# Cluster attention and token mixing: score operands kept in the rows where casts write them, and the two heads of a pair in the two halves of TensorE's rows

## The chip, the cores and the metric

The kernel runs on one core of one Trainium2 chip. The metric is the device time of one execution in microseconds; the number for the kernel before is the median of three runs. All arithmetic of the reference is done on the core; the host only transposes and reshapes inputs and output.

## The reference

```python
# q, k, v: (4, 8, 768, 64); centroids: (8, 16, 64); batch 4, 8 heads, 768 tokens
q_assign = np.argmax(np.einsum('bhsd,hcd->bhsc', q_n, c_n), axis=-1)
k_assign = np.argmax(np.einsum('bhsd,hcd->bhsc', k_n, c_n), axis=-1)
mask = q_assign[:, :, :, None] == k_assign[:, :, None, :]
scores = scale * np.matmul(q, k.transpose(0, 1, 3, 2))
scores = np.where(mask, scores, -1000000000.0)
scores = scores - np.max(scores, axis=-1, keepdims=True)
attn = np.exp(scores)
attn = attn / (np.sum(attn, axis=-1, keepdims=True) + 1e-09)
attn_out = np.matmul(attn, v)
...
# x: the eight heads side by side, (4, 768, 512)
theta = x @ w_theta
cos_t, sin_t = (np.cos(theta), np.sin(theta))
zr = x * cos_t
zi = x * sin_t
yr = np.einsum('ts,bsd->btd', w_tok_r, zr)
yi = np.einsum('ts,bsd->btd', w_tok_i, zi)
u = x + yr + yi
return u + np.maximum(u @ w_ch, 0.0)
```

Each query attends only to keys whose nearest centroid is its own. The inputs are float32, and w_theta and w_tok_i are scaled by about 5.5.

## The kernel before

**Stages.** Attention comes first, for 16 pairs of heads (two heads of one batch, 64 channels each, so a pair fills 128 rows). Then token mixing runs batch by batch: theta in six tiles of 128 tokens (`theta`, L602), the two mixing products (`mix`, L677), and the channel product with its relu (`channel`, L719). Values that need float32's precision are split into a high and a low float32r part (hi, lo) whose products are added in PSUM: hi·hi + hi·lo + lo·hi.

**One pair.** Its 768 x 768 scores are cut into twelve *units*: two halves a of 384 queries by six tiles i of 128 keys. A unit holds both heads j. `scores` (L356) makes for each head a 128 x 384 tile of scores with keys in rows, and ScalarE's exponential writes it to `at` (L367). GpSimd adds the `at` of three units into `acc` (L374). `weighted` (L405), three units later (`LAG`), multiplies by v into `av`, two units at a time. `sums` (L376) adds the columns of `acc` on TensorE into `sm`; `se` is the sum, VectorE inverts it (L394, 128 x 384), a DMA writes four rows of it to DRAM (`sd`, L397), two more read it back to all rows (`rb`, L400), and `normalise` (L419) multiplies and stores the pair to `xT_d`. These stages stand at the units `SUMS` and `NORM` of the next pair.

**Shift and mask in the product.** A one-hot of the 16 clusters, scaled by 2^60 on the side of the keys, is part of the product's rows: a pair of tokens of one cluster adds 0, any other a huge negative number. The row maximum that is subtracted comes from a cheaper product of hi parts with queries in rows (`row_max`, L325, tile `m`), which VectorE reduces (L341) into `nm`; `shift_row` (L345) transposes `nm` (tile `mt`), and a DMA puts it as one row into the score operands. `row_max` runs `LEAD` = 11 units ahead of `scores`, and shift rows are made four units ahead of their first use (five for the first pair).

**Operand tiles.** TensorE sums over up to 128 rows in one product. hi·hi (64 rows), parts of the other terms and the 16 one-hot rows are packed for each head into t1q/t1k (112 rows: 64 of hi·hi, 32 of hi·lo, 16 of one-hot) and t2q/t2k (97 rows: lo·hi, the rest of hi·lo, the shift row against a row of ones). So a score tile takes two products, and a maximum, which uses t1 alone, takes one for each half of the keys. Casts write hi and lo in rows (head, channel); `spread` (L307) moves them into place with 16 DMAs per pair on SyncE's queue, and four more (L272) move the one-hot rows.

**Assignment.** `assign` (L217) loads q and k of a pair, multiplies with the normalised centroids (`lg`, four column groups), transposes (`lt`, three transposes), takes the maximum on VectorE, breaks ties, writes the one-hot `oh`, transposes it in six steps into `ot`, and one ScalarE instruction of 64 x 768 writes it to `oht` (L265). Its stages stand at units `A_UNITS` of earlier pairs.

**Order.** The code writes instructions unit by unit, and `in_order` (L457) chains those of one engine in just that order. In the loop at L525 each unit issues score products and maxima of both heads in turn, then `weighted`, then whatever `todo` holds for the unit. In the units before the first score TensorE also gets two idle products a step (`WARM`).

**PSUM.** Of eight banks four are two double banks for `m`, one is `av`, and three (tag "bank") serve sc, lg, lt, ot, mt and sm in turn.

**Weights.** Float weights arrive as pairs of 32-bit words of float64, which VectorE and ScalarE turn into float32 (`to_f32`, L112), and `split_w` cuts into hi and lo. `early_weights` (L428) does eight chunks (w_theta, and two of six tiles each of w_r and w_i) beside attention, 18 units apart. `late` (L585) does the other w_r and w_i, and w_ch in eight chunks of 256 columns, while batch 0 mixes.

## Time and profile before

| what | value |
|---|---|
| median of 3 runs | 863.19 us (862.38 to 864.5) |
| the profiled execution | 865.01 us, of which 863.2 us are the span in the profile |
| mean granted TensorE clock | 0.976 |
| busy time by stage, 0 to 43 us (before the first score) | PE 24.59, VectorE 18.32 |
| 43 to 490 us (attention) | PE 429.74 of 447, VectorE 311.38, GpSimd 326.59, ScalarE 253.62 |
| 490 to 600 us | PE 94.86 of 110, VectorE 92.84 |
| HBM | read 45.15 MB, written 12.68 MB |

How to read it: the span runs from the first to the last instruction. PE is TensorE's products and PEld its loads of stationary operands, which overlap products. A busy PE need not be at its peak, because a product's end is modelled and includes the drain of the array; the distance between the starts of two products is what a step costs. An engine's mean share hides that the stages have different limits, so each stage is read by itself. "sc<-t1q,t1k" is a product that writes the tile sc from the operands t1q and t1k, and L365 is its line.

### The profile page before, as it was taken

What the parts mean: (1) busy time and instruction counts of PE and PEld (TensorE: products, weight loads), DVE (VectorE), ACT (ScalarE), POOL (GpSimd) and SP (SyncE); (2) the same over time, 40 slices, a digit from 0 to 9 for tenths busy, and PEclk for the clock granted to TensorE, in tenths of its full rate; (3) what the DMA queues carried; (4) which work ended last, traced back from release to release, by engine and by line L of the source; (5) the groups of instructions that cost most, each with busy time, mean ns of one, the idle gap of its engine ahead of it and who ended that gap; (6) DMA issues with size and microseconds to landing.
All of it is one profiled execution on the core that took longest, in us unless ns stands there. A gap on an engine that the chain in (4) does not pass through costs nothing.

```text
span 863.2 us, 12659 instructions
## 1 busy us (share of the span) xinstructions
PE 809.2 (94%) x4637; PEld 596.4 (69%) x4637; DVE 513.4 (59%) x665; ACT 398.9 (46%) x798; POOL 470.4 (54%) x303
## 2 busy tenths in 40 slices
PE   3799999999998989999999999868999999999998
PEld 1476565656565656565656678658888988899998
DVE  4476768786766687776654498994323442344222
ACT  3155565556554655565555655452333333333220
POOL 4157776977596668876867555546122512251231
PEclk9899999999998999999999999997999999999999
DMA  8856658675877496757631154321200120010001
GB/s 204 207 149 155 177 143 195 178 187 150 183 188 169 124 218 157 200 143 180 165 102 56 38 185 145 89 83 55 93 1 1 51 96 2 1 45 29 1 13 63
DMA packets 44942, 99.67 MB, mean 115 GB/s; under 512 B 8400, under 2 KB 19408, under 8 KB 44496
## 3 DMA queue, kind: packets, MB, share of 16 engines
q1 hardware_dynamic: 44288, 98.27, 42.8%
q8 instruction: 37, 0.61, 0.3%
q10 hardware_dynamic: 592, 0.59, 0.3%
q14 instruction: 25, 0.20, 0.1%
HBM read 45.15 MB, written 12.68 MB: 67 GB/s over the span
## 4 chain that ended last, share of the span: by engine, by line
PE 60%; DMA 13%; DVE 12%; issue 4%; ACT 4%; SPq 3%; POOL 2%; ACTq 0%; POOLq 0%; DVEq 0%
PE y L687 18%; PE sc L365 10%; PE av L411 9%; PE tp L620 6%; PE m L337 5%; PE cy L710 4%; DMA t2k<-rawk 3%; PE cp L710 3%; DMA t1k<-hik 2%; PE sm L384 2%; SPq L317 2%; DMA rawk<-in_kT_dram 2%; DVE wtmp L135 2%; POOL acc L374 2%; DMA rb<-sd 1%
## 5 line engine op out<-in xcount | busy, mean ns | idle before, releaser
L341 DVE TENSOR_REDUCE nm<-m 128x1 f32<-128x768 f32 x192 | 180.8, 950 | 134.8 <-PE m L337 131.8
L367 ACT ACTIVATE at<-sc 128x384 f32<-128x384 f32 x384 | 178.3, 491 | 129.7 <-PE sc L365 104.1
L374 POOL TENSOR_TENSOR acc<-at,at 128x768 f32<-128x768 f32 x64 | 120.0, 1875 | 101.5 <-ACT at L367 101.3
L365 PE MATMUL sc<-t1q,t1k 112*128 112x384 f32 x384 | 146.6, 382 | 8.5 <-ACT oht L265 4.4
L411 PE MATMUL av<-at,vt 128*64 128x384 f32 x768 | 147.5, 506 | 0.0
L337 PE MATMUL m<-t1k,t1q 112*128 112x384 f32 x384 | 139.2, 363 | 7.9 <-DVE nm L341 5.3
L365 PE MATMUL sc<-t2q,t2k 97*128 97x384 f32 x384 | 132.6, 345 | 2.5 <-DMA t2q<-mr 2.4
L374 POOL TENSOR_TENSOR acc<-acc,at 128x768 f32<-128x768 f32 x64 | 121.6, 1901 | 18.2 <-ACT at L367 15.5
L365 PEld LDWEIGHTS sc<-t1q,t1k 112*128 112x128 f32 x384 | 73.6, 192 | 69.4 <-issue 33.1
L641 POOL TENSOR_TENSOR zlc<-ab,zhc 128x512 fp32r<-128x512 f32 x24 | 32.1, 1336 | 162.1 <-ACT zhc L639 162.1
L411 PEld LDWEIGHTS av<-at,vt 128*64 128x64 f32 x768 | 47.2, 137 | 59.7 <-issue 59.5
L337 PEld LDWEIGHTS m<-t1k,t1q 112*128 112x128 f32 x384 | 77.3, 201 | 12.1 <-DVE nm L341 7.7
L365 PEld LDWEIGHTS sc<-t2q,t2k 97*128 97x128 f32 x384 | 73.6, 192 | 3.7 <-DMA vt<-in_v_dram 2.7
L624 DVE TENSOR_SCALAR kk<-tp 128x512 int32<-128x512 f32 x24 | 16.5, 686 | 93.8 <-PE tp L620 93.8
L701 POOL TENSOR_TENSOR ul<-xT,uh 128x384 fp32r<-128x384 f32 (+1 forms) x36 | 33.8, 963 | 34.4 <-ACT uh L700 34.2
L687 PE MATMUL y<-wi_hi,zls 128*128 128x512 f32 (+1 forms) x216 | 52.4, 321 | 0.0
L687 PE MATMUL y<-wr_hi,zlc 128*128 128x512 f32 (+1 forms) x216 | 52.3, 320 | 0.0
L687 PE MATMUL y<-wr_lo,zhc 128*128 128x512 f32 (+1 forms) x216 | 52.1, 320 | 0.0
L687 PE MATMUL y<-wr_hi,zhc 128*128 128x512 f32 (+1 forms) x216 | 52.0, 319 | 0.0
L687 PE MATMUL y<-wi_lo,zhs 128*128 128x512 f32 (+1 forms) x216 | 52.0, 319 | 0.0
L687 PE MATMUL y<-wi_hi,zhs 128*128 128x512 f32 (+1 forms) x216 | 52.0, 319 | 0.0
L615 ACT COPY xn<-xp 128x512 f32<-128x512 f32 x24 | 14.0, 584 | 78.4 <-PE xp L613 78.4
(138 smaller groups left out, 1414.6 us busy)
## 6 DMA issues: line engine op xcount, KB each, us to landing
rawq<-in_qT_dram SPq DMA_DIRECT2D x16, 384.0 KB
t1k<-hik SPq DMA_DIRECT2D x32, 192.0 KB
t2k<-hik SPq DMA_DIRECT2D x32, 192.0 KB
t1q<-hiq SPq DMA_DIRECT2D x32, 192.0 KB
t2q<-rawq SPq DMA_DIRECT2D x32, 192.0 KB
vt<-in_v_dram SPq DMA_DIRECT2D x16, 384.0 KB
rb<-sd SPq DMA_DIRECT2D x32, 192.0 KB
xT_d<-xt SPq DMA_DIRECT2D x16, 384.0 KB
```

Source lines behind the costliest of these rows:

```text
L135: nc.vector.scalar_tensor_tensor(out=wi, in0=low, scalar=29, in1=wi, op0=ALU.logical_shift_right, op1=ALU.bitwise_or)
L337: nc.tensor.matmul(m[:, c, 0:HS], lhsT=s["t1q"][0:KM, j, t * P:(t + 1) * P], rhs=s["t1k"][0:KM, j, c * HS:(c + 1) * HS], start=True, stop= ...
L341: nc.vector.tensor_reduce(out=s["nm", a][:, j, i // 2:i // 2 + 1], in_=m[:, :, 0:HS], op=ALU.max, axis=AX.XY, negate=True)
L365: nc.tensor.matmul(sc, lhsT=s[x][0:kk, j, i * P:(i + 1) * P], rhs=z, start=(x == "t1k"), stop=(x == "t2k"))
L367: last_exp[0] = nc.scalar.activation(out=at[:, j], in_=sc, func=AF.Exp, scale=SCALE)
L374: last_acc[0] = nc.gpsimd.tensor_tensor(out=s["acc", a, x], in0=prev, in1=at, op=ALU.add)
L411: nc.tensor.matmul(s["av"][64 * j:64 * j + 64], lhsT=s["vt"][:, i, j, :], rhs=s["at", a, i][:, j], start=(i == 0), stop=(i == NT - 1))
L620: nc.tensor.matmul(tp, lhsT=xx[:, c, :], rhs=w_th[c][k], start=(n == 0), stop=(n == 3 * NCT - 1))
L641: nc.gpsimd.tensor_tensor(out=zl, in0=tr, in1=zh.bitcast(F32), op=ALU.subtract)
L687: nc.tensor.matmul(y_at(b, d, c0, c1), lhsT=zz[:, d * P:(d + 1) * P], rhs=ww[:, c0:c1], start=first and lead, stop=last, skip_group_check= ...
L701: nc.gpsimd.tensor_tensor(out=ul[:, d, :], in0=x, in1=uh[:, d, :].bitcast(F32), op=ALU.subtract)
L710: nc.tensor.matmul(cp, lhsT=w_c[d][k][:, e * P:(e + 1) * P], rhs=uu[:, d, :], start=(n == 0), stop=(n == 3 * NCT - 1), skip_group_check=True)
```

## The change

The six operand tiles of a pair (hq, lq, hk, lk: hi and lo of q and k; mq, mk: the masks) now have 128 rows with head 0 in rows 0 to 63 and head 1 in rows 64 to 127, which is how casts and the assignment write them. `spread` and the one-hot DMAs are gone. The products run over 64 rows: four for a score tile (hi·hi, lo·hi, hi·lo, mask) and two for each half of a row maximum (hi·hi, mask), and `heads` issues the two heads' products in turn, one in rows 0 to 63 and one in rows 64 to 127, with separate output banks. The one-hot lies in rows 0 to 15 and 64 to 79 of the mask tiles, and the shift row in rows 32 and 96, against ones that the bias `mbi` puts there.

Other edits in the diff:

- one `row_max` every second unit, for both heads, in two tiles m; `LEAD` 10 instead of 11, `LAG` 2 instead of 3, `NAT` (buffers of at) 6 instead of 5
- the one-hot is made in 64 columns per group (`ohp`), transposed in two visits of six, and copied by two ScalarE instructions of 128 x 768
- the sums are written to DRAM, read back as 128 x 12, inverted there, written again and read back to all rows; `SUMS` has five stages instead of four, and `NORM` stands one unit later
- the shift row goes out as two DMAs, five units ahead of its use
- four buffers for the raw q and k; a plain preparation of the first pairs in the common loop
- w_ch is split with the early weights: twelve chunks, 15 units apart

```diff
-LEAD = 11
+LEAD = 10
...
-SUMS = (2, 4, 5, 7)
-NORM = (10, 12)
+SUMS = (2, 3, 5, 7, 9)
+NORM = (11, 13)
...
-LAG = 3
-NAT = 5
+LAG = 2
+NAT = 6
...
+    w_c = [hi_lo(wpool, f"wch{c}", DM) for c in range(NCT)]
...
-        tsets[x] = {n: pt.tile([P, 2, S], F32R, name=f"{n}_{x}") for n in ("t1q", "t1k", "t2k")}
-        tsets[x]["t2q"] = pt.tile([P, 2, 2, HS], F32R, name=f"t2q_{x}")
+        tsets[x] = {n: pt.tile([P, S], F32R, name=f"{n}_{x}") for n in ("hq", "lq", "hk", "lk", "mq", "mk")}
...
-        ot = bank(f"ot{pi}").bitcast(BF16)[0:4 * C, 0:S]
...
-        nc.scalar.activation(
-            out=oht, in_=ot, func=AF.Identity, scale=msc[0:4 * C], bias=mbi[0:4 * C])
...
+        for n, x in enumerate(("mq", "mk")):
+            yield
+            ot = bank(f"ot{pi}{n}").bitcast(BF16)[:, 0:S]
+            for t in range(NT):
+                a, y = divmod(t, NH)
+                nc.tensor.transpose(out=ot[:, t * P:(t + 1) * P], in_=ohv[:, 2 * y + a, n], identity=identb)
+            if n == 0:
+                nc.scalar.copy(out=st[pi][x], in_=ot)
+            else:
+                nc.scalar.activation(out=st[pi][x], in_=ot, func=AF.Identity, scale=BIG, bias=mbi)
...
+    def heads(*products):
+        for n, (outs, stat, cols, mov, over) in enumerate(products):
+            for j in range(2):
+                r = slice(64 * j, 64 * j + 64)
+                nc.tensor.matmul(
+                    outs[j], lhsT=stat[r, cols], rhs=mov[r, over],
+                    start=(n == 0), stop=(n == len(products) - 1))
...
+        m = [ps0.tile([P, 2, 512], F32, tag="m", name=f"m{u}_{j}") for j in range(2)]
+        q = slice(t * P, (t + 1) * P)
+        for c in range(2):
+            k = slice(c * HS, (c + 1) * HS)
+            outs = [m[j][:, c, 0:HS] for j in range(2)]
+            heads((outs, s["hq"], q, s["hk"], k), (outs, s["mq"], q, s["mk"], k))
...
+        sc = [bank(f"sc{u}_{j}")[:, 0:HS] for j in range(2)]
+        k, q = slice(i * P, (i + 1) * P), slice(a * HS, (a + 1) * HS)
+        heads(*((sc, s[x], k, s[z], q) for x, z in (("hk", "hq"), ("hk", "lq"), ("lk", "hq"), ("mk", "mq"))))
+        for j in range(2):
+            last_exp[0] = nc.scalar.activation(out=at[:, j], in_=sc[j], func=AF.Exp, scale=SCALE)
...
-        nc.vector.reciprocal(out=se, in_=se)
+        nc.sync.dma_start(out=sd[0], in_=se.rearrange("(g r) n -> g r n", r=32)[:, 0])
+        yield
+        sq = p2.tile([P, 4 * HS // P], F32, tag="sq", name=f"sq{pi}")
+        nc.sync.dma_start(out=sq, in_=over[0])
+        yield
+        nc.vector.reciprocal(out=sq, in_=sq)
+        nc.sync.dma_start(out=over[1], in_=sq)
...
+        for c in range(NCT):
+            yield from split_w(*w_c[c], w_ch[c * P:(c + 1) * P], DM, raw_pair, nc.gpsimd, CKE)
...
-    A_UNITS = (-6, -4, -3, -1, 2, 8, 9)
-    W_EVERY = 2
+    A_UNITS = (-2, 2, 4, 5, 6, 8, 9)
+    HI_UNITS = dict(q=0, k=1)
+    LO_UNITS = dict(q=2, k=4)
+    W_EVERY = 15
...
-        for x in range(2):
-            if 0 <= u < NUT:
-                scores(u, x)
-            if 0 <= u + LEAD < NUT:
-                row_max(u + LEAD, x)
+        if 0 <= u < NUT:
+            scores(u)
+        if u % 2 == 0 and u + LEAD < NUT:
+            row_max(u + LEAD)
```

The first place is TensorE in the fifth pair (units 49 and 50, away from other stages). The last number of a name counts instructions; sc49_0 is unit 49's score tile of head 0, m60 the maximum of unit 60. Before:

```order
L365 MATMUL sc49_0_1596<-t1q_1_123,t1k_1_124 128x384
L365 MATMUL sc49_0_1596<-t2q_1_126,t2k_1_125 128x384
L337 MATMUL m60_1601<-t1k_2_131,t1q_2_130 128x384
L365 MATMUL sc49_1_1603<-t1q_1_123,t1k_1_124 128x384
L365 MATMUL sc49_1_1603<-t2q_1_126,t2k_1_125 128x384
L337 MATMUL m60_1601<-t1k_2_131,t1q_2_130 128x384
```

Now, from the last two products of each head's scores in unit 50 to the end of unit 60's maxima:

```order
L300 MATMUL sc50_0_1836<-hq_1_131,lk_1_134 128x384
L300 MATMUL sc50_1_1837<-hq_1_131,lk_1_134 128x384
L300 MATMUL sc50_0_1836<-mq_1_135,mk_1_136 128x384
L300 MATMUL sc50_1_1837<-mq_1_135,mk_1_136 128x384
L300 MATMUL m60_0_1850<-hk_2_142,hq_2_140 128x384
L300 MATMUL m60_1_1851<-hk_2_142,hq_2_140 128x384
L300 MATMUL m60_0_1850<-mk_2_145,mq_2_144 128x384
L300 MATMUL m60_1_1851<-mk_2_145,mq_2_144 128x384
L300 MATMUL m60_0_1850<-hk_2_142,hq_2_140 128x384
L300 MATMUL m60_1_1851<-hk_2_142,hq_2_140 128x384
L300 MATMUL m60_0_1850<-mk_2_145,mq_2_144 128x384
L300 MATMUL m60_1_1851<-mk_2_145,mq_2_144 128x384
```

The scores of the two heads now end next to each other instead of three products apart, and the maxima stand in a block of eight at even units instead of one product after every two.

The second place is TensorE around the transposes `lt` of pair 6's assignment. Before:

```order
L365 MATMUL sc45_1_1513<-t2q_0_140,t2k_0_139 128x384
L337 MATMUL m56_1511<-t1k_1_124,t1q_1_123 128x384
L242 MATMUL lt6_1525<-identf_64,lgs6_1502 128x128 x3
L365 MATMUL sc46_0_1534<-t1q_0_137,t1k_0_138 128x384
L365 MATMUL sc46_0_1534<-t2q_0_140,t2k_0_139 128x384
```

Now:

```order
L300 MATMUL m62_0_1917<-mk_2_145,mq_2_144 128x384
L300 MATMUL m62_1_1918<-mk_2_145,mq_2_144 128x384
L241 MATMUL lt6_1929<-identf_64,lgs6_1878 128x128 x3
L300 MATMUL sc53_0_1939<-hq_1_131,hk_1_133 128x384
L300 MATMUL sc53_1_1940<-hq_1_131,hk_1_133 128x384
```

The transposes use all 128 rows; their neighbours used 97 to 112 rows before and use 64 now, and the place is seven units later.

The third place is VectorE while batch 0's last tiles are mixed: kk and r are theta's range reduction of batch 1, wtmp are weights on their way to float32, those of 256 columns w_ch. Before:

```order
L624 TENSOR_SCALAR kk1_0_5617<-tp1_0_5604 128x512
L609 TENSOR_TENSOR xl1_2_6008<-xT1_5591,xh1_2_6007 128x512
L130 TENSOR_SCALAR wtmp_5636<-wtmp_5636 128x256
L137 SCALAR_TENSOR_TENSOR wtmp_5534<-wtmp_5534 128x384
L626 SCALAR_TENSOR_TENSOR r1_0_5619<-kk1_0_5617,tp1_0_5604 128x512
L132 TENSOR_SCALAR wtmp_5636<-wtmp_5636 128x256
L627 SCALAR_TENSOR_TENSOR r1_0_5619<-kk1_0_5617,r1_0_5619 128x512
L135 SCALAR_TENSOR_TENSOR wtmp_5636<-wtmp_5636 128x256
L130 TENSOR_SCALAR wtmp_5645<-wtmp_5645 128x256
L137 SCALAR_TENSOR_TENSOR wtmp_5636<-wtmp_5636 128x256
```

Now:

```order
L586 TENSOR_SCALAR kk1_0_6630<-tp1_0_6617 128x512
L571 TENSOR_TENSOR xl1_2_6949<-xT1_6604,xh1_2_6948 128x512
L588 SCALAR_TENSOR_TENSOR r1_0_6632<-kk1_0_6630,tp1_0_6617 128x512
L589 SCALAR_TENSOR_TENSOR r1_0_6632<-kk1_0_6630,r1_0_6632 128x512
L598 TENSOR_TENSOR ab1_0_6635<-ab1_0_6635,xn1_0_6615 128x512
L598 TENSOR_TENSOR r1_0_6632<-r1_0_6632,xn1_0_6615 128x512
```

The pieces of w_ch between theta's instructions are gone from here; they stand among attention's instructions now.

More of the change, by code (lines that the diff above doesn't have):

```diff
@@ L215 @@
     NG = HS // C
+    ohp = pe.tile([P, NG, 64], BF16, name="ohp")
+    nc.vector.memset(ohp, 0.0)
     wb = wc.unsqueeze(1).broadcast_to([P, NG, C])
@@ L283, in load_v @@
         nc.sync.dma_start(out=st[pi]["vt"], in_=v[b, p])
[L289 to L295 removed]
     def part_hi(pi, n):
         s = st[pi]
[L299 to L300 removed]
+        nc.scalar.copy(out=s["h" + n], in_=s["raw" + n])
     def part_lo(pi, n, eng):
         s = st[pi]
[L304 to L317 removed]
+        eng.tensor_tensor(out=s["l" + n], in0=s["raw" + n], in1=f(s["h" + n]), op=ALU.subtract)
     NU = 2 * NT
+    NH = NT // 2
     def split_u(u):
@@ L582 @@
         w_i[t] = hi_lo(pool, f"wi{t}", S)
-    w_c = [hi_lo(m0, f"wch{c}", DM) for c in range(NCT)]
     def late():
@@ L591, in late @@
             yield
-        for c in range(NCT):
-            for gen in split_w(*w_c[c], w_ch[c * P:(c + 1) * P], DM, wt_pair, nc.gpsimd, CK):
-                run(gen)
-            if c % 2:
-                yield
     zs = {}
```

171 lines of the change are left out of this document (51 added, 120 removed).

## Prediction

> **What bounds the kernel now.** I read the page's shares first, then the slices, the busy table by stage, the timeline of TensorE in one quiet stretch, the chain that ended last for the pitch of the pairs, and the groups by line and shape for durations.
>
> ```profile
> PE 809.2 (94%) x4637; PEld 596.4 (69%) x4637; DVE 513.4 (59%) x665; ACT 398.9 (46%) x798; POOL 470.4 (54%) x303
> 480.00:600.00 120.00, 104.86 (x528) 83.87 (x527) 97.10 (x156) 61.95 (x123) 69.65 (x55) 0.91 0.33 103
> 600.00:860.00 260.00, 260.00 (x1632) 238.39 (x1630) 90.45 (x161) 78.98 (x138) 65.95 (x60) 1.00 0.09 33
> ```
>
> TensorE is the bound, but not everywhere alike. From 600 us on it is full at full clock and the change touches nothing, so some 258 us stay. In 480 to 600 it has holes (104.86 of 120, clock 0.91) while VectorE is busy 97.10. Before 490 stands attention, where the steps of TensorE look like this (start, duration, tile):
>
> ```profile
> 107.72 1.51 PE L411 MATMUL av<-at,vt 128*64 128x384 f32 x8
> 109.16 0.44 PE L365 MATMUL sc<-t1q,t1k 112*128 112x384 f32 x1
> 109.44 0.34 PE L365 MATMUL sc<-t2q,t2k 97*128 97x384 f32 x1
> 109.62 0.34 PE L337 MATMUL m<-t1k,t1q 112*128 112x384 f32 x1
> ...
> 111.22 0.33 PE L337 MATMUL m<-t1k,t1q 112*128 112x384 f32 x1
> 111.49 1.51 PE L411 MATMUL av<-at,vt 128*64 128x384 f32 x8
> ```
>
> Two units take 111.49 - 107.72 = 3.77 us: twelve products (eight sc, four m) at (111.22 - 109.44)/10 = 0.178 from start to start, 1.44 of weighted sums (107.72 to 109.16), and the rest where the width of the tile changes. A record's own duration includes its drain; the distance of starts is the price. The pitch of the pairs (twelve units, one "sm" each) is in the chain:
>
> ```profile
> 74.28 1.47 PE sm L384 x16
> ...
> 244.91 1.43 PE sm L384 x16
> ...
> 258.87 9.24 DMA t2q<-mr
> ...
> 277.60 1.47 PE sm L384 x16
> ...
> 417.63 1.43 PE sm L384 x16
> ...
> 471.29 1.43 PE sm L384 x16
> ```
>
> The last two pairs, which split no weights, take (471.29 - 417.63)/2 = 26.8 us each; the twelve before them (417.63 - 74.28)/12 = 28.6, so 21 us too much in all. One pair alone, with the late shift row of 9.24 us, takes 32.7, 4 above that mean. I put 6 us in all to late transfers and the other 15 to the eight weight chunks, 1.9 each.
>
> **Part 1, products over 64 rows: taken as nothing.** Per two units the scores go from eight products to sixteen and the maxima from four to eight, but they come in pairs on rows 0-63 and 64-127 with outputs in different banks. If a pair runs side by side it is one step, and there are twelve steps again. No row of before has two row halves at work. The nearest are the column groups of the assignment logits:
>
> ```profile
> 200.56 0.49 PE L411 MATMUL av<-at,vt 128*64 128x384 f32 x2
> 200.99 0.27 PE L349 MATMUL mt<-identf,nm 128*6 128x128 f32 x1
> 201.19 0.52 PE L263 MATMUL ot<-identb,oh 128*64 128x128 bf16 x6
> 201.64 0.51 PE L233 MATMUL lg<-rawq,cb 128*32 128x384 f32 x1
> 201.65 0.51 PE L233 MATMUL lg<-rawk,cb 128*32 128x384 f32 x1
> ...
> 201.99 0.49 PE L233 MATMUL lg<-rawq,cb 128*32 128x384 f32 x1
> ...
> 202.43 0.44 PE L365 MATMUL sc<-t1q,t1k 112*128 112x384 f32 x1
> 202.71 0.34 PE L365 MATMUL sc<-t2q,t2k 97*128 97x384 f32 x1
> ```
>
> Four products start within 0.02 us and the next four 0.35 later, so four column groups do run together; and the first, whose four stationary loads nothing hides, last only 0.02 longer, so their loads overlap too. I carry that over to row halves as an estimate: 0 us. The ends: the eight av of 107.72 go through in four steps, (1.51 - 0.49)/3 = 0.34 each with the first load, 0.32 without, and each reads its 384 columns for two passes, so 0.16 a pass. If paired scores reach that, 12 x 0.018 x 96 double units = -20 us; if nothing runs together, 12 x 0.178 x 96 = +205 us.
>
> **Part 2, changes of tile shape: +1.5 us per pair, +24.** The rows above give the price: such a step is 0.32, but 0.43 before another shape (200.56 to 200.99, 201.99 to 202.43), so 0.10 of drain, and the next product follows after 0.28 instead of 0.18, 0.10 of load that nothing hides. Now sc and m have the same shape as the transposes; after the change they have 64 rows, and mt, lt and ot stand alone between them.
>
> The Trainium skill, "TensorEngine Tiling (Array Packing)", Key Properties, says that changing the tiling mode, not just the tile, drains TensorE. The 0.10 us agrees for columns; no run here shows it for rows. If rows were free of it, this part would be about half.
>
> ```profile
> 203.72 0.45 PE L365 MATMUL sc<-t1q,t1k 112*128 112x384 f32 x1 [0.49 <-ACT oht L265]
> ...
> 204.18 0.34 PE L337 MATMUL m<-t1k,t1q 112*128 112x384 f32 x1
> 204.35 0.49 PE L242 MATMUL lt<-identf,lgs 128*128 128x128 f32 x3
> 204.60 0.42 PE L365 MATMUL sc<-t1q,t1k 112*128 112x384 f32 x1
> ```
>
> The three lt cost 0.42 - 0.18 = 0.24 now; with a change on either side 0.38 more. Each mt, now 0.03 beyond the change that av has anyway, gets a change of its own: 0.2, twice per pair. The ot go from six transposes (0.056 each, in a row with lg) to two visits of six: 0.73 more. Sum 0.38 + 0.4 + 0.73 = 1.5. Bounds 0.6 to 2.0 per pair.
>
> **Part 3, waits for PSUM banks: +0.2 us per pair, +3.**
>
> ```profile
> 109.88 0.97 ACT L367 ACTIVATE at<-sc 128x384 f32<-128x384 f32 x2 [1.73 <-PE sc L365]
> L367 ACT ACTIVATE at<-sc 128x384 f32<-128x384 f32 x384 | 178.3, 491 | 129.7 <-PE sc L365 104.1
> L341 DVE TENSOR_REDUCE nm<-m 128x1 f32<-128x768 f32 x192 | 180.8, 950 | 134.8 <-PE m L337 131.8
> L394 DVE RECIPROCAL se<-se 128x384 f32<-128x384 f32 x16 | 40.7, 2541 | 1.2 <-ACT se L390 1.2
> ...
> 143.20 3.77 DMA rb<-sd
> ```
>
> Three banks serve scores, and both heads of a unit now end together. An exponential starts 0.44 after its last product starts (109.44 to 109.88) and takes 0.49. From the start S of an even unit: last step S+0.63, first exponential done S+1.56, its bank usable again with its load about S+1.72; the odd unit wants it at S+1.51 (0.63 + five steps of 0.178). That is 0.21 lost, in about three of six odd units (mt, lt, ot shift the banks), plus about 0.45 where lt's bank waits for VectorE and where ScalarE's second, full-height mask copy precedes an exponential: near 1.4 per pair, against some 1.2 that such waits cost now (the 0.49 at 203.72 is one; the 26.8 of a clean pair, less its steps, leaves about that). Bounds -0.6 to +1.2. The maxima come in bursts of two reductions, 1.9 of every 3.75 us; VectorE may be about 3 us late with other work before TensorE waits, so pairs without weights stay clear. The 2.54 us reciprocal becomes one over 12 columns: -0.3 per pair, -5. For that the sums pass through DRAM twice, and two instructions wait anew: the reciprocal, with the next reductions behind it on VectorE and TensorE's maxima behind those, and POOL's normalisation, with the next pair's adds behind it. Each transfer has two units, 3.75 us; the larger one in the chain took 3.77 with the old queue, so I take 0, and 0.5 per pair as the far end.
>
> **Part 4, weights: +3 us here, -13 later.** Twelve chunks instead of eight are split in attention. VectorE loses the reciprocal that collides with them, so I take 1.5 instead of 1.9 each: 18 - 15 = +3 (bounds -3 to +8). Late transfers: -6, because the spread of parts (t1, t2) leaves the queue and the shift row gets five units instead of four. Later, batch 0's channel stage loses its w_ch splits:
>
> ```profile
> 576.59 0.51 PE L687 MATMUL y<-wi_hi,zls 128*128 128x256 f32 x2
> 605.31 0.60 PE L613 MATMUL xp<-identf,xT 128*128 128x128 f32 x4
> 674.66 0.51 PE L687 MATMUL y<-wi_hi,zls 128*128 128x256 f32 x2
> 691.67 0.60 PE L613 MATMUL xp<-identf,xT 128*128 128x128 f32 x4
> ```
>
> From the last mixing product to the next batch's transposes it takes 28.7 us; batch 1, the same program with no splits beside it, 17.0. Gain 11.7, and about 1.3 in the stretch ahead, where VectorE was behind: -13 (bounds -6 to -16). The holes that w_r and w_i leave stay.
>
> **Part 5, start: -11 us.**
>
> ```profile
> 12.96 0.99 ACT L265 ACTIVATE oht<-ot,mbi,msc 64x768 fp32r<-64x768 bf16 x1 [4.66 <-PE ot L263]
> 19.16 0.66 PE L337 MATMUL m<-t1k,t1q 112*128 112x384 f32 x1 [2.44 <-DMA t1q<-oht]
> 32.43 5.29 DMA rawk<-in_kT_dram
> 43.20 0.67 PE L365 MATMUL sc<-t1q,t1k 112*128 112x384 f32 x1
> ```
>
> The first maximum waits for DMAs of the one-hot rows. Without them two copies of 0.99 follow each other, and it starts near 12.96 + 1.98 = 15. From there to the first score it is 24 us, of which the load of pair 2 (32.43), whose logits stand ahead in TensorE's order, holds 5.3. Then five bursts remain, each about 1.3 (four steps at the cold clock) + 0.4 + 1.9 = 3.6, the last without its reductions: 15.7, and about 1.3 for pair 1's assignment on VectorE. First score at 32 instead of 43 (bounds 30 to 37).
>
> **Sum.** Start -11; attention 24 + 3 - 5 + 3 - 6 = +19; later -13: -5 us. The profiled execution took 865.0 (863.2 of span and 1.8 around it) and stands 1.8 above the median of 863.2, so 865.0 - 5 - 1.8 = **858 us**.
>
> **Rivals.**
> - *Steps shorter* (12%). Pairs stream at 0.16 as av does: 20 us less, 838. For it: those rows. Against: av reads each element for two passes, these for one.
> - *Lumps win* (16%, slower). One mechanism: with three banks and both heads ending at once, the next unit waits on the exponential in all six odd units and after each of the seven other bank users, so the mean pair grows by 1.3 us over my sum: 879. The sign turns where the mean pair in attention is 1.5 us above today's 28.4, since 24 us of gains stand against sixteen pairs. For it: ScalarE's 0.49 at 203.72. Against: 129.7 us of slack before the exponentials.
> - *Stationary loads in line* (8%). If the two loads of a pair can't overlap, a step is two loads of 0.10 plus their issue, 0.21: 0.032 x 12 x 96 = +37 us, 895.
> - *The halves don't run together* (6%), so the change doesn't do what it says: 858 + 205 = 1063 us.
>
> By the Trainium skill, "TensorE: Matmul & The Clock Gate", Measured speedup vs the span model, four row tiles gave 3.07 times one tile's rate, not four; an estimate from that, 0.178 x 4/3.07 = 0.232 per pair, would give 62 us more, 920. No run here shows it, and its measurement is of one short group.
>
> **Numbers.** The forecast has 58%, with its own range 845 to 871, wider than its errors in single terms (start 4, tile shapes 11, banks 11, weights 5). A measurement can tell 0.3%, 2.6 us, from no change. Of the forecast's 58, 39 lie below 860.6, 12 within, 7 above; with the shorter steps that is 51% faster, 12% same, 7 + 16 + 8 + 6 = 37% slower. The range 836 to 890 leaves out the two cases of halves that don't overlap and some tails, under 20%.
>
> **What would show it.** Starts of paired products a few ns apart and the next pair 0.18 later: part 1. A first score near 32 us; a pair without weights near 28.2; the gap between batch 0's last mixing product and the next transposes near 17 us; mt and lt 0.2 to 0.4 dearer; no DMA in front of a score. It is wrong if score pairs start 0.2 or more apart, or if waits for "ACT at" ahead of sc grow past 1.5 us per pair.

## The result, and the profile after

The changed kernel takes 884.79 us (884.09 to 886.23), the kernel before 862.8 on the same chip: a ratio of 1.0253, with a 95% interval of 1.0233 to 1.0273. It is 22 us slower. The forecast was 858, in a range of 836 to 890 that holds the time; the most likely sign was wrong. The profiled execution has a span of 882.3 us at a mean clock of 0.983.

The page of the changed kernel first, its shares and the lines of the chain that ended last; then its busy time by the stages of the table above (stretch, its length, then busy us of PE, PEld, VectorE, ScalarE and GpSimd).

```profile
PE 820.8 (93%) x5861; PEld 605.2 (69%) x5861; DVE 473.7 (54%) x650; ACT 399.1 (45%) x806; POOL 468.5 (53%) x297
...
PE y L649 19%; PE sc L300 15%; PE av L394 12%; PE tp L582 6%; PE m L300 5%; PE cy L672 4%; DVE nm L319 4%; ACTq L332 3%; PE cp L672 2%; PE lg L232 2%; ACT at L345 2%; PE ot L262 1%; DVE eq L250 1%; PE xp L575 1%; PE y L672 1%
```

```profile
0.00:43.00 43.00, 27.81 (x198) 17.43 (x200) 21.95 (x48) 15.90 (x28) 14.65 (x16) 0.96 0.33 106
43.00:490.00 447.00, 416.62 (x3400) 258.07 (x3396) 276.05 (x310) 241.09 (x518) 316.49 (x172) 0.98 0.25 78
```

VectorE has less to do in attention than before (276 against 311), and TensorE has more holes there (30 us of 447 against 17). The chain shows where to look: 4% of the span is VectorE's maxima (nm), and 3% is "ACTq L332", the issue of the shift row's DMAs on ScalarE's queue. Neither is among the lines that the page of before lists for its chain.

The quiet stretch of the changed kernel answers to the one of the prediction (start, time from the first start to the last end of the group, number):

```profile
117.85 1.51 PE L394 MATMUL av<-at,vt 128*64 128x384 f32 x8
119.29 0.44 PE L300 MATMUL sc<-hq,hk 64*128 64x384 f32 x2
119.58 0.34 PE L300 MATMUL sc<-lq,hk 64*128 64x384 f32 x2
119.75 0.34 PE L300 MATMUL sc<-hq,lk 64*128 64x384 f32 x2
...
120.62 0.34 PE L300 MATMUL m<-mk,mq 64*128 64x384 f32 x2
120.79 0.55 PE L300 MATMUL sc<-hq,hk 64*128 64x384 f32 x2
...
121.79 0.54 PE L394 MATMUL av<-at,vt 128*64 128x384 f32 x2
```

Pairs of products start together (two take 0.34, as one does) and follow each other after 0.17. Two units take 121.79 - 117.85 = 3.94 instead of 3.77. The odd unit's first two start apart: both together last 0.55, since the second one waits about 0.1 for its bank, which the even unit's first exponential reads until 120.84 (the load for that product begins at 120.90).

Where the time went, by the starts of five instructions in each trace (the last column is a version found by the experiments):

| us | before | change | later and on SyncE | the same, weights at unit 3 |
|---|---|---|---|---|
| first score | 43.2 | 30.0 | 30.0 | 29.6 |
| from there to the sums of the first pair | 31.0 | 36.4 | 32.9 | 31.7 |
| 13 pairs, sums to sums | 369.5 | 397.2 | 378.9 | 361.6 |
| from there to the first mixing product | 60.1 | 69.0 | 64.4 | 65.5 |
| from there to the end | 359.4 | 349.8 | 349.5 | 349.9 |
| span | 863.2 | 882.3 | 855.7 | 838.2 |

The start gained 13 and mixing 10; the 13 pairs lost 28, the first pair 5, the way to mixing 9. TensorE's waits in attention, by what ended them (us in all, times, longest), first before, then after:

```profile
PE m L337 <- DVE nm L341: 5.3, 5, 1.2
PE sc L365 <- ACT oht L265: 4.4, 10, 0.7
PE sc L365 <- ACT at L367: 2.8, 4, 1.2
```

```profile
PE mt L327 <- DVE nm L319: 19.2, 9, 4.2
PE sc L300 <- ACT at L345: 7.9, 13, 1.2
PE lg L232 <- ACT at L345: 2.8, 7, 1.0
```

One wait is new: the transpose `mt`, with which a shift row begins, waits 19.2 us for VectorE's maxima. And the waits for exponentials went from 2.8 to 10.7.

### The profile page after: what moved, and what is told of

Same layout as the page of the kernel before. It is cut to its first block, busy times and chain, and to the rows that moved or that the text cites. A ratio compares the mean times of both kernels' runs of the same rounds, so it can differ in the third digit from the quotient of the medians.

```text
span 882.3 us, 14586 instructions
## 1 busy us (share of the span) xinstructions
PE 820.8 (93%) x5861; PEld 605.2 (69%) x5861; DVE 473.7 (54%) x650; ACT 399.1 (45%) x806; POOL 468.5 (53%) x297
## 4 chain that ended last, share of the span: by engine, by line
PE 72%; DVE 13%; issue 4%; ACT 4%; ACTq 3%; DMA 2%; POOL 1%; SPq 0%; POOLq 0%; DVEq 0%
PE y L649 19%; PE sc L300 15%; PE av L394 12%; PE tp L582 6%; PE m L300 5%; PE cy L672 4%; DVE nm L319 4%; ACTq L332 3%; PE cp L672 2%; PE lg L232 2%; ACT at L345 2%; PE ot L262 1%; DVE eq L250 1%; PE xp L575 1%; PE y L672 1%
## 5 line engine op out<-in xcount | busy, mean ns | idle before, releaser
L319 DVE TENSOR_REDUCE nm<-m 128x1 f32<-128x768 f32 x192 | 174.6, 950 | 166.5 <-PE m L300 166.3
L345 ACT ACTIVATE at<-sc 128x384 f32<-128x384 f32 x384 | 167.5, 489 | 137.7 <-PE sc L300 123.6
L394 PE MATMUL av<-at,vt 128*64 128x384 f32 x768 | 144.8, 499 | 0.0
L300 PE MATMUL sc<-hq,hk 64*128 64x384 f32 x384 | 97.5, 430 | 9.8 <-ACT at L345 9.7
L300 PEld LDWEIGHTS sc<-hq,hk 64*128 64x128 f32 x384 | 48.9, 185 | 68.0 <-ACT at L345 57.3
L300 PE MATMUL sc<-lq,hk 64*128 64x384 f32 x384 | 80.0, 345 | 0.0
L300 PE MATMUL sc<-hq,lk 64*128 64x384 f32 x384 | 77.1, 338 | 0.0
L300 PE MATMUL sc<-mq,mk 64*128 64x384 f32 x384 | 76.9, 336 | 0.0
L300 PE MATMUL m<-hk,hq 64*128 64x384 f32 x384 | 69.1, 347 | 1.2 <-DVE nm L319 1.2
L300 PE MATMUL m<-mk,mq 64*128 64x384 f32 x384 | 68.5, 345 | 0.4 <-ACT mk L266 0.4
```

The source lines that it names most:

```text
L300: nc.tensor.matmul(outs[j], lhsT=stat[r, cols], rhs=mov[r, over], start=(n == 0), stop=(n == len(products) - 1))
L319: nc.vector.tensor_reduce(out=s["nm", a][:, j, i // 2:i // 2 + 1], in_=m[j][:, :, 0:HS], op=ALU.max, axis=AX.XY, negate=True)
L345: last_exp[0] = nc.scalar.activation(out=at[:, j], in_=sc[j], func=AF.Exp, scale=SCALE)
L394: nc.tensor.matmul(s["av"][64 * j:64 * j + 64], lhsT=s["vt"][:, i, j, :], rhs=s["at", a, i][:, j], start=(i == 0), stop=(i == NT - 1))
```

## The experiments

Each is the changed kernel with the edit shown, unless its text says otherwise. Ratios stand against the kernel before on the same chip, where it takes 861.4 to 863.2 us, so a difference between times from two chips is good to about 2 us.

### Theta's tiles, the shift row, w_ch, and a step between units

Four first suspicions, one for each place that had lost time. Pools for xT around theta's small tiles:

```diff
-    mx = mctx.enter_context(tc.tile_pool(name="mx", bufs=2))
+    mxa = mctx.enter_context(tc.tile_pool(name="mxa", bufs=1))
     ma = mctx.enter_context(tc.tile_pool(name="ma", bufs=2))
+    mxb = mctx.enter_context(tc.tile_pool(name="mxb", bufs=1))
...
-        xT = mx.tile([P, NP, S], F32, tag="xT", name=f"xT{b}")
+        xT = (mxb if b % 2 else mxa).tile([P, NP, S], F32, tag="xT", name=f"xT{b}")
```

> The changed kernel with one edit: the two buffers of xT are allocated in two pools around theta's small tiles, so that theta's casts lie again in memory of pair 13's operands and not of pairs 14 and 15; ScalarE's order then has four of batch 0's six casts xh among the last pair's exponentials instead of all six behind them. Theory A (theta starts late because of where its tiles lie): the first mixing product follows the last score by about 11 to 13 us instead of 23.7, and the time falls by 9 to 13 us, to 872 to 876. Rival B (the hand-over is long because late weights load late, whatever the order of casts): no change, 882 to 887.

884.47 us, ratio 1.0247: no change, the number of rival B (whose reason, late weights, the run doesn't show). Theory A's sign did come: the first mixing product follows the last score by 8.2 us (530.44 - 522.26). Three of theta's sums run before the last score again, but the last pairs grow by as much. Work that TensorE does in either place is not lost where it is late; the landmark of the first mixing product had misled.

```diff
-            at_unit(u + a * NT - LEAD + NT - 1, shift_row, pi, a)
+            at_unit(u + a * NT - LEAD + NT, shift_row, pi, a)
```

> The changed kernel with each shift row one unit later, four units ahead of its use instead of five. Theory A (TensorE stands at the transpose mt because VectorE is behind with the maxima when weights are split beside them; excess at mt 21 us in all, seven stalls of 0.6 to 4.3): each stall shrinks by up to one unit, 1.95 us, the time falls by about 12 us, to 870 to 875. Rival B (VectorE is so far behind that TensorE then waits at the next maxima's banks instead): under 3 us less, 881 to 885.

860.25 us, ratio 0.9969 (0.9949 to 0.9988): 24.5 us less, twice what theory A gave, from one unit. The wait at mt is gone:

```profile
PE m L300 <- DVE nm L319: 9.4, 11, 2.4
PE sc L300 <- ACT at L345: 2.4, 6, 0.5
```

Half of it came back at the maxima's banks (rival B, 9.4), but the waits for exponentials fell too, from 10.7 to 2.4, and a pair without any stall by VectorE became 1.1 us shorter. Theory A has no reason for that.

```diff
     def early_weights():
...
-        for c in range(NCT):
-            yield from split_w(*w_c[c], w_ch[c * P:(c + 1) * P], DM, raw_pair, nc.gpsimd, CKE)
...
-    W_EVERY = 15
+    W_EVERY = 18
...
     def late():
...
+        for c in range(NCT):
+            for gen in split_w(*w_c[c], w_ch[c * P:(c + 1) * P], DM, wt_pair, nc.gpsimd, CK):
+                run(gen)
+            if c % 2:
+                yield
```

> The changed kernel with w_ch split late again as before the change: eight early chunks 18 units apart, eight late ones of 256 columns. Theory A (a chunk beside attention costs 2.4 us since it delays the maxima and with them mt): attention about 10 us shorter, batch 0's channel stage 11 to 12 us longer, time 883 to 889. Rival B (a chunk costs the 1.5 us of the prediction, and the stalls at mt are from something else): attention 6 us shorter, time 888 to 893. Rival C (with VectorE more than half idle in attention a chunk costs nothing): 894 to 897.

885.26 us, ratio 1.0254: theory A. The 13 pairs take 387.7 instead of 397.2, and first mixing product to end 361.6 instead of 349.8. So a chunk cost 2.4 in attention, and early or late w_ch came out even.

```diff
...
-            heads((outs, s["hq"], q, s["hk"], k), (outs, s["mq"], q, s["mk"], k))
+            heads((outs, s["hq"], q, s["hk"], k), (outs, s["mq"], q, s["mk"], k),
+                  *(((outs, zst, slice(0, P), s["mk"], k),) if c == 1 else ()))
```

> The changed kernel with one more pair of products per two units, of zeros, added to the second half of the maxima: TensorE has a step of 0.172 more between the scores of an even and of an odd unit; the values stay. Theory A (the odd unit's second head waits about 0.1 us for a PSUM bank that the exponential still reads, and pays another 0.1 for a load that nothing hides then): the step fills the hole, the time changes by -4 to +4 us, 881 to 889. Rival B (no hole there): 0.172 x 96 = 16.5 us more, 899 to 903.

885.09 us, ratio 1.0263: theory A. Six more steps of 0.172 per pair lengthen the shortest pairs by 0.2 to 0.3. So most of each step falls into a hole ahead of the odd unit's scores.

### Two units later, heads apart, the full reciprocal, and another visit

```diff
-            at_unit(u + a * NT - LEAD + NT - 1, shift_row, pi, a)
+            at_unit(u + a * NT - LEAD + NT + 1, shift_row, pi, a)
```

> The changed kernel with each shift row two units later, three ahead of its use, so again at odd units, behind the weighted sums, as in the change itself. VectorE has a unit more than with one unit later. Theory A (the 24.5 us that one unit later gained come from VectorE's time alone): a pair without stalls stays at 27.6 to 27.9, the time is 854 to 861. Theory B (about 1.1 us per pair of it comes from the place: at an even unit the transpose stands in the hole ahead of the odd unit's scores and costs little, at an odd unit it stands between the weighted sums and the next scores and costs a change of shape of its own): a clean pair is back at 28.6 to 28.9, the waits of mt for VectorE stay gone, the time is 870 to 878.

884.22 us, ratio 1.0267. The 24.5 us are lost again, and more than theory B gave: the sums around one of the shortest pairs stand at 95.64 and 125.21, 29.57 apart. TensorE's waits in attention:

```profile
PE sc L300 <- ACT mk L266: 9.8, 14, 0.7
PE m L300 <- DVE nm L319: 7.8, 10, 2.6
PE sc L300 <- ACT at L345: 5.3, 18, 0.6
```

mt no longer waits for VectorE, so time for VectorE (theory A) is not what a clean pair, one without such stalls, had gained. But a hole in TensorE's order does not explain waits for ScalarE either. ScalarE's own row of the changed kernel does:

```profile
109.93 0.25 ACT L329 CAST mr<-mt 6x128 fp32r<-6x128 f32 x1
110.21 1.41 ACTq L332 DMA_DIRECT2D mq<-mr  x2
111.72 0.87 ACT L345 ACTIVATE at<-sc 128x384 f32<-128x384 f32 x2 [1.54 <-PE m L300]
```

and in the kernel before there was this:

```profile
105.73 0.68 ACTq L353 DMA_DIRECT2D t2q<-mr  x1
```

The two DMAs of a shift row are issued from ScalarE's queue and hold it for 1.41 us, where one held it for 0.68. At an odd unit the issue falls just when the next even unit's exponentials could start (the last products of its scores begin at 110.29 and last 0.34); they start at 111.72. Their banks come free late, and the transposes ot and the odd unit's scores wait. That was theory C of the next runs.

```diff
-        for n, (outs, stat, cols, mov, over) in enumerate(products):
-            for j in range(2):
+        for j in range(2):
+            for n, (outs, stat, cols, mov, over) in enumerate(products):
```

> The changed kernel with the products of a unit in another order: all of head 0 and then all of head 1, so that neighbours use the same half of TensorE's rows, except where the head changes. Theory A (the two halves do run side by side, and products in one half follow each other every 0.172 us): two units take 17 steps instead of 12, five more, 0.86 less the 0.2 of hole that is filled: 60 to 83 us more in 96 double units, 945 to 968. Rival B (a pair takes 0.172 because of something else than the two halves): within 10 us of 885.

One run, 880.1 us, in rival B's range: the step count of theory A is far off. The program has four products of head 0 and then four of head 1, and the trace still shows

```profile
120.26 0.46 PE L300 MATMUL sc<-hq,hk 64*128 64x384 f32 x2
120.54 0.35 PE L300 MATMUL sc<-lq,hk 64*128 64x384 f32 x2
120.71 0.35 PE L300 MATMUL sc<-hq,lk 64*128 64x384 f32 x2
```

Head 1's first product, fifth in the program, starts within 0.02 us of head 0's first. TensorE ran ahead in the free half, so this edit leaves open what the halves do; another one had to tell.

```diff
-SUMS = (2, 3, 5, 7, 9)
-NORM = (11, 13)
+SUMS = (2, 4, 5, 7)
+NORM = (10, 12)
...
+        nc.vector.reciprocal(out=se, in_=se)
+        yield
+        sd = dram.tile([4, HS], F32, tag="sd", name=f"sd{pi}", bufs=2)
+        nc.sync.dma_start(out=sd, in_=se.rearrange("(g r) n -> g r n", r=32)[:, 0])
```

> The changed kernel with the sums as before the change: VectorE inverts 128 x 384 (2.54 us per pair) and one trip through DRAM. Theory A (VectorE's time counts twice where mt waits for it): clean pairs 0.3 to 1 us longer, stalls in pairs with weights longer, 5 to 16 us more, 890 to 901. Rival B (VectorE has room where the reciprocal stands, and the second trip costs as much as it brings): 882 to 888.

904.31 us, ratio 1.0498: the direction of theory A and more than its range. The waits of mt for VectorE rise from 19.2 to 30.1, and a clean pair takes 30.2. While mt stands where it does, 2.54 us more of VectorE come with 1.2 us more time per pair (19.5/16), though the edit also takes out one trip through DRAM and moves `NORM`; 10.9 of the 19.5 are waits of mt.

The next one has the shift row one unit later, and besides:

```diff
-    A_UNITS = (-2, 2, 4, 5, 6, 8, 9)
+    A_UNITS = (-2, 2, 4, 5, 6, 8, 10)
```

> The changed kernel with the shift row one unit later and with the second visit of the one-hot's transposes at unit 10 instead of 9, so that all visits of other tiles stand at even units, ahead of the odd unit's scores. Theory A (such a visit costs less there, because the odd unit's scores would wait for a bank anyway): 0.2 to 0.4 us less in each of 15 pairs, 3 to 6 us, 854 to 857.5. Rival B (the hole is used up by the other visits of that unit, or the place makes no difference): 858.5 to 862.

864.16 us, ratio 1.0025 (1.0002 to 1.0047), 4 us more than with the shift row alone: both theories fall, and that even units are the better place as such is wrong. Why this visit costs more at unit 10 wasn't followed further.

### The issue on SyncE, and both products in one half

```diff
-            nc.scalar.dma_start(
+            nc.sync.dma_start(
                 out=f(s["mq"][64 * j + 32:64 * j + 33, a * HS:(a + 1) * HS]).rearrange("o (t n) -> o t n", n=P),
```

> The changed kernel with the two DMAs of each shift row issued by SyncE instead of ScalarE. Theory C (the issue of two DMAs holds ScalarE's queue for 1.41 us, twice per pair, just when the even unit's exponentials could start; their banks come free late, and the scores and the transposes of the one-hot behind them wait): a clean pair falls from 28.75 by 0.8 to 1.2, and the time by 13 to 20, to 865 to 872, with the stalls of mt for VectorE still there. Rival D (the exponentials have slack, and one unit later gained only by VectorE's time): a clean pair stays at 28.6 to 28.9, 881 to 887.

868.97 us, ratio 1.0093 (1.0076 to 1.0109): theory C. ScalarE at the place shown above:

```profile
108.66 0.25 ACT L329 CAST mr<-mt 6x128 fp32r<-6x128 f32 x1
109.45 0.87 ACT L345 ACTIVATE at<-sc 128x384 f32<-128x384 f32 x2 [0.54 <-PE sc L300]
```

The exponential follows as soon as scores are there. A clean pair (sums at 123.00 and 150.64) takes 27.64, and mt's wait for VectorE is still 19.0, so the two causes are separate.

Then both edits to the shift row together, this one and the one unit:

> The changed kernel with the shift row one unit later and its DMAs issued by SyncE. Theory C: at even units the issue mostly lies where ScalarE waits for the odd unit's scores, so little is left to gain over 860: 0 to 0.5 us per pair, 852 to 860. Rival D (the place does it by a hole in TensorE's order): no gain over 860, 858 to 862.

858.14 us, ratio 0.9971 (0.9952 to 0.999), 27 us less than the change (24 by the ratios). The time lies in both ranges, and beside one unit later alone (ratio 0.9969) SyncE adds nothing; that the issue counts is shown by the run before, at the old place. Both edits together leave a clean pair at 27.59 (90.55 to 118.14), and of the waits 9.7 for maxima in pairs with chunks. The shift row later by one unit had worked twice: VectorE got time, and the issue moved behind the even unit's exponentials.

The halves by themselves:

```diff
-                r = slice(64 * j, 64 * j + 64)
+                r = slice(0, 64)
```

> The changed kernel with both products of every pair on rows 0 to 63, so that head 1's scores and maxima are computed from head 0's operands. Theory A (the two halves of the rows run side by side, each with a product every 0.172, and TensorE runs ahead in the half that is free, which is why the order of the heads did not matter): 24 steps instead of 12 in two units, 2.06 us more less about 0.2 of hole, 178 to 198 us more in 96 double units, 1060 to 1085. Rival B (a product of 64 rows costs half of one of 112 to 128 rows in any half): within 15 us of 885.

1034.99 us in one run, 150 more than the change: the direction of theory A, its size by more waits filled than I had counted (a clean pair goes from 28.76 to 39.36, 1.77 per two units where twelve more steps are 2.06). In one half products go one by one, 0.174 apart (two take 0.50):

```profile
118.26 0.50 PE L300 MATMUL m<-hk,hq 64*128 64x384 f32 x2
118.61 0.51 PE L300 MATMUL m<-mk,mq 64*128 64x384 f32 x2
```

So the halves are what makes a pair of products cost one.

And narrower chunks, on top of both edits to the shift row:

```diff
-    CKE = S
+    CKE = HS
...
-        return (pw.tile([P, 2 * CKE], F32, tag="w64", name="w64"), pw.tile([P, CKE], F32, tag="w32", name="w32", bufs=1))
+        return (pw.tile([P, 2 * CKE], F32, tag="w64", name="w64"), pw.tile([P, CKE], F32, tag="w32", name="w32", bufs=2))
...
-    W_EVERY = 15
+    W_EVERY = 7
```

> As the run with the shift row one unit later and on SyncE, with the early weights in chunks of half the width, 7 units apart. Theory A (what is left of the pairs with weights, stalls of 2 to 2.7 us of the maxima for VectorE, comes from its long instructions standing together): lumps of half the size, 4 to 9 us less than that run, about 848 to 853. Rival (VectorE's total work in the pair counts, which grows by the fixed part of more instructions): 0 to 5 us more than that run.

866.04 us, ratio 1.007: 8 us more than with whole chunks. The rival in direction, with more than it gave; its reason isn't shown, since 24 chunks 7 units apart also stand at other places. TensorE's waits for maxima stay at 9.9.

### The place of the weight chunks

In the run with both edits the pairs differed by 6.6 us. The good ones had their chunk's VectorE instructions at units 7 and 11 or 10 and 2, the bad ones at 1 and 5 or 4 and 8, and the assignment's are at 4, 5 and 6. VectorE in the changed kernel, ahead of a wait of mt, and the transpose itself:

```profile
164.00 1.17 DVE L250 TENSOR_TENSOR eq<-eq,wc 128x384 bf16<-128x384 bf16 x1
165.20 0.55 DVE L252 TENSOR_REDUCE rr<-eq 128x24 bf16<-128x384 bf16 x1
165.67 1.74 DVE L133 SCALAR_TENSOR_TENSOR w<-w,w 128x512 int32<-128x512 int32 x1
167.44 2.18 DVE L135 SCALAR_TENSOR_TENSOR w<-w,w 128x512 int32<-128x512 int32 x1
169.54 1.81 DVE L319 TENSOR_REDUCE nm<-m 128x1 f32<-128x768 f32 x2
```

```profile
171.50 0.27 PE L327 MATMUL mt<-identf,nm 128*6 128x128 f32 x1 [3.69 <-DVE nm L319]
```

```diff
-    W_EVERY = 15
+    W_EVERY = 12
...
-        u = W_EVERY * x
+        u = W_EVERY * x + 3
```

With the two edits to the shift row, and chunks begun at unit 3 or at unit 0:

> As the run with the shift row one unit later and on SyncE (858.1), with one weight chunk per pair, begun at unit 3, so that its VectorE instructions stand at units 7 and 11, clear of the assignment's at 4, 5 and 6. Theory A (a chunk costs only where its VectorE instructions stand next to the assignment's, and the maxima behind both): the pairs' excess of 20 us over 27.6 falls below 6, the time is 838 to 846. Rival B (VectorE's total work counts, about 1.7 us per chunk wherever it stands): every pair 1.5 to 2 us longer than 27.6, 855 to 861.

> The same with the chunk begun at unit 0, so that its VectorE instructions stand at units 4 and 8, the first of them with the assignment's. Theory A: every pair with a chunk and an assignment is one of the bad ones, 2 to 5 us more each, 865 to 895. Rival B: as with chunks at unit 3, 855 to 861.

840.29 us, ratio 0.9743 (0.9715 to 0.9771), and 871.27, ratio 1.01 (1.0067 to 1.0133). The same twelve chunks, 31 us apart by their place. With chunks at unit 3 (first line) TensorE hardly waits for maxima, with chunks at unit 0 (second) it does all along:

```profile
PE m L300 <- DVE nm L319: 0.4, 1, 0.4
```

```profile
PE m L300 <- DVE nm L319: 16.9, 25, 2.2
```

These waits are not all of the 31 us, because TensorE's granted clock drops behind long waits. In the changed kernel, behind the transpose shown above, a step takes 0.17 at first and then 0.32, while the clock (0.50, third number from the end) is at half; with chunks at unit 3 (second row of the second block) it is 1.00 from 30 to 470 us:

```profile
172.15 0.34 PE L300 MATMUL sc<-hq,lk 64*128 64x384 f32 x2
172.32 0.34 PE L300 MATMUL sc<-mq,mk 64*128 64x384 f32 x2
...
172.76 0.53 PE L300 MATMUL m<-mk,mq 64*128 64x384 f32 x2
173.08 0.53 PE L300 MATMUL m<-hk,hq 64*128 64x384 f32 x2
```

```profile
172.60:176.00 3.40, 3.40 (x24) 2.52 (x20) 1.82 (x2) 2.15 (x4) 1.38 (x1) 0.50 0.53 144
30.00:470.00 440.00, 436.60 (x3627) 268.86 (x3625) 299.77 (x319) 258.36 (x558) 337.40 (x182) 1.00 0.28 88
```

With chunks at unit 0 four such stretches, 20.4 us in all, begin at the end of waits of 2.2 us for maxima or up to 2.7 us later; at 0.32 instead of 0.17 per step that is about 10 us more (an estimate). So what a bad place costs is the wait and the clock behind it; no run separates the two, and not every long wait has such a stretch behind it (the one of 2.1 us at 358.5 in the change has none). The change and the run with both edits have 13.6 us each at half clock in the pairs.

Is that also the whole of mt's wait in the change? The same place for the chunks, and nothing else:

> The changed kernel with one weight chunk per pair, begun at unit 3, and nothing else changed: the shift row stays where the change puts it, issued by ScalarE. Theory A (the waits of mt for VectorE, 19.2 us, exist only where a chunk's VectorE instructions stand by the assignment's): they fall below 4, a clean pair stays at 28.7, the time is 862 to 870. Rival B (mt one unit behind the last maxima is too early in any case): mt still waits 10 us or more, 874 to 885.

875.27 us, ratio 1.0132: rival B's time, and a wait between the theories. mt's wait for VectorE falls from 19.2 to 6.1, so most of it was the chunks' place and some is there in any case; another 6.1 of its waits now end with ScalarE's copy of av (1.1 in the change). The waits of sc for exponentials rise from 7.9 to 15.9 (17 times), and pairs with chunks take 29.9: the chunks' ScalarE instruction (L127, begun at 110.84) now stands between the issue of the shift row (109.32 to 110.73) and the exponentials (begun at 111.40).

Last, the kernel before, with one chunk per pair begun at unit 2 and, in the second run, at unit 4:

```diff
-        u = 3 * NU * x // W_EVERY
+        u = NU * x + 2
```

> The kernel before with one weight chunk per pair, begun at unit 2, so that its VectorE instructions stand at units 6 and 10, clear of the assignment's at 9, 11 and 2. Theory A (the place of the chunks is worth as much in the old structure as in the new one, where it brought 18): 845 to 852. Rival B (in the old structure a chunk costs about 1.5 wherever it stands, since transposes and maxima stand further apart): 860 to 865.

> The same with the chunk begun at unit 4, its VectorE instructions at units 8 and 0. Theory A: 845 to 852. Rival B: 860 to 865.

893.58 us, ratio 1.0352, and 853.87, ratio 0.9887 (0.9866 to 0.9908). Theory A in direction, just outside its range; the first place is a bad one that I had taken for a good one, 40 us from the second. These 40 are not VectorE's alone: over the 13 pairs of the table TensorE waits 12.4 for maxima at the bad place, but also 9.2 for the shift row's DMA (0 and 0.4 at the good one), and its granted clock is 0.91 from 72 to 292 us, which costs about 20 us (an estimate: at half clock for 18% of 220 us, with half of that lost), while at the good place it is 1.00 from 60 to 490. In the good place the old operands reach 853.87, the new ones with all three edits 840.29. One place of two was good here and others weren't tried, so the 13.6 between them (12.4 by the ratios) compare two places as much as two layouts of operands.

## Why the prediction was wrong, point by point

**What held.** The first score came at 30.0 (32 forecast), the start gained 13 (11). Paired products run side by side at 0.17, shown by the run with both in one half; the estimate from column groups carried over, and the 0.16 of the shorter steps didn't come (0.173, against 0.178 before). A transpose mt between two shapes takes 109.66 - 109.46 = 0.20 in the trace, as forecast, and the second visit of six ot 115.42 - 114.98 = 0.44, of 0.73 forecast for both visits. Batch 0's channel stage takes 17 us. The later part gained 9.6 of 13.

**The step that failed** is in parts 3 and 4: "the shift row gets five units instead of four", counted as a gain among 6 us of late transfers, and "VectorE may be about 3 us late with other work before TensorE waits". The limit of 3 us was that of the maxima's banks. But the transpose mt needs the last burst of the same maxima, and the change puts it one unit behind that burst, where it had two before. An earlier consumer of the same result ended VectorE's slack, and the earlier place that I booked as a gain was the loss. It cost 19.2 us of waits, of which the later shift row brought 11 net (868.97 to 858.14). Most of them need the chunks at their place as well (6.1 with chunks at unit 3), and so the term for the chunks failed with it: a chunk cost 2.4 in the change (9.5 for four), not 1.5.

**What I did not price** is the second shift DMA. The working counts what leaves SyncE's queue and prices the two trips of the sums, but ScalarE's queue appears nowhere, though the issue was in the trace of before with 0.68. Twice 1.41 per pair, in front of exponentials: 16 us (884.8 to 869.0; 14 by the ratios).

Together these are 27 us, and without them the kernel takes 858.14, the forecast to the digit. That is luck: on that chip the kernel before is 2 us faster too, so the ratio is 0.997 and not 0.994, and the terms were off against each other (start 13 gained instead of 11, attention 16 lost instead of 19, later 10 gained instead of 13, by the table; 4 of the 16 lie on the way to mixing and weren't followed). The clean pair of 26.8 came from the last two pairs, which lack nearly all of an assignment (no pair follows them) while the second has theta's first products; between two others of before it is 130.47 - 103.42 = 27.05. Set against that, the change without the two faults costs 0.5 per pair and not 1.4 (27.59 - 27.05); 0.3 of the difference are 72 steps of 0.173 instead of 0.178. The price of a chunk is no constant: nearly 0 at unit 3 and over 2 at unit 0, half clock included. And the reciprocal, -5, brings 19.5 in the change as it stands, more than half of it at mt.

The forecast has no term for the granted clock. The pair of 32.7, which it puts down to a late shift row, shows one: TensorE waits 2.4 us there, and then its clock is 0.50 from 268.1 to 274.9.

**The rivals.** "Lumps win" named 879 and late exponentials, and these did come, from 2.8 to 10.7 us of waits. Its mechanism was another one, though: with both heads ending at once two quiet units grew by only 0.17 (3.94 against 3.77), bank wait included, and what made most of the lumps was a queue (3.2 us of the 10.7 are left with the issue on SyncE). No rival had mt. Neither sign that was to show the forecast wrong came: pairs of products start 0.17 apart, and sc waits 7.9/16 = 0.5 us per pair for exponentials.

## What to carry to other kernels

For a wait that a change moves, look for the earliest consumer of what the late engine makes, not the one whose buffer holds longest; here one unit of place was worth 24 us, 11 of them by this wait and most of the rest by the issue that moved with it. Count each DMA that a change adds on the queue of the engine that issues it: where that engine's next work feeds a ring of three banks, part of the issue is on the path (about 0.5 of 1.41 us here, 16 us over 32 visits). And a side job split over a repeated pattern has no fixed price; put it at one place of the pattern and try the places, since the same twelve chunks took 840 or 871 us. A wait can cost more than its length: look at the granted clock behind it.

## What the runs showed of the hardware that I had not expected

- TensorE runs ahead in the half of its rows that is free: with four products of one half in front in the program, the other half's first started within 0.02 us of the first. The Trainium skill, "TensorE: Matmul & The Clock Gate", The mechanism, says that products keep the program's order in start and end, and that only loads are pulled ahead; the trace of the run with heads apart differs, across row halves.
- A product over 64 rows costs the same 0.174 as one over 97 to 112 rows (0.178) when its half is the only one at work.
- The issue of one small DMA takes ScalarE 0.7 us (0.69, and SyncE as long). The Trainium skill, "DMA: Bandwidth & Descriptors", Issuing engines are not separate DMA queues, calls the time that an engine spends on initiating a DMA usually small beside the transfer; here moving the issue to SyncE was worth 14 to 16 us.
- A chunk's integer steps on VectorE (two inputs, 128 x 512) seem to wait for whole instructions of GpSimd: L133, begun at 165.67 in the changed kernel, lasts 1.74 and ends 0.55 after an add that GpSimd ran from 164.90 to 166.86; L135, begun at 167.44, ends about 0.54 after the next add (167.19 to 169.08). The maxima, 0.95 with one input from PSUM, don't show it. No run tried this by itself.
